# Padding the last 64-token key and query block of each batch to the full 128 x 128 TensorE array

## The chip, the cores and the metric

The kernel runs on one core of one Trainium2 chip. The metric is device time in microseconds (us), lower is better. PE is TensorE, DVE VectorE, ACT ScalarE, POOL GpSimd. PV is the product of the attention weights P with the values v. In the trace a matmul is a weight load (LDWEIGHTS) and a MATMUL. "128*64" is the part of the array it uses: 128 rows (contraction) by 64 columns (output partitions, the width of the loaded weights). The shape behind it, such as 128x65, is the streamed operand: 65 columns.

Single runs of one kernel agree to within about 1%.

## The reference, cut to what matters

Sliding-window attention with an ALiBi bias (8 batches, 8 heads, 576 tokens, head size 64, window 128), then a two-layer feed-forward with squared relu (4608 tokens, 512 to 2048 to 512):

```python
scores = scale * np.matmul(q, k.transpose(0, 1, 3, 2))        # 8 x 8 x 576 x 576
mask = (rel >= 0) & (rel < 128)                               # rel = query pos - key pos
attn = softmax(np.where(mask, scores + bias, -1e9))
x = np.matmul(attn, v) -> reshape to (4608, 512)
out = (np.maximum(x @ w_in, 0) ** 2) @ w_out
```

576 is 4.5 times 128: every batch ends in a block of 64 keys and 64 queries. That half block is the subject.

## The kernel before

A small list scheduler fixes the order of all instructions ahead of time. It interleaves the attention of the coming batches with the feed-forward of tokens already finished. Per batch there are 5 key blocks, the last with n = 64. Cuts are marked with `...`.

```python
blk = [min(128, S - kb * 128) for kb in range(NKB)]          # 128,128,128,128,64
...
for kb in range(NKB):
    n, nq = blk[kb], qcols[kb]
    for c in range(C):                                       # 4 pairs of heads
        nc.tensor.matmul(                                    # scores: n weight columns
            slot.tile[0:n, 0:2 * nq]...,
            kT[p2][c][:, kb * 128:kb * 128 + n],
            qp[p2][c][:, :, kb * 128:kb * 128 + nq], start=True, stop=True)
        # ACT: P = exp(scale * scores) on n partitions; DVE: P = P * masks
    for hf in range(2):
        for hi in range(4):                                  # PV: 8 heads, up to two key blocks each
            for (sp, kk, off) in parts:                      # previous block, this block
                nk = blk[kk]
                nc.tensor.matmul(
                    slot.tile[0:n, hi * (D + 1):(hi + 1) * (D + 1)],
                    sp.tile[0:nk, h, off:off + n],           # weights: nk rows, n columns
                    vt[i][0:nk, kk, h, :], start=st, stop=en)
        # DVE: reciprocal of the row sum, x = pv * reciprocal
    for c in range(C):                                       # transposes of x: n rows
        nc.tensor.transpose(slot.tile[:, c * 128:c * 128 + n],
                            sx.tile[0:n, c * 128:(c + 1) * 128], ident[0:n, 0:n])
```

In the last block of a batch, n = 64 gives 4 score matmuls of form 128*64, 8 PV matmuls of 128*64 (previous key block), 8 PV matmuls of 64*64 (last key block) and 4 transposes of 64*128. That is 24 per batch and 192 in the kernel. P and x come from rotating pools (`work.tile`).

The softmax here doesn't subtract the row's maximum and nothing guards it: scores larger than these inputs give would overflow.

Of the kernel before, what the change touches and what calls it, by code (L numbers as in the profile page):

```python
# [30 lines left out]
class Slot:  # L31


    def __init__(self, tag):
        self.tag, self.tile, self.left, self.freed = tag, None, 0, 0.0


class Plan:
# [17 lines left out]
    def order(self):  # L56
        used = {tag: [] for tag in self.bufs}
        free = {}
        cand = {}
        left = {}  # L60
        for t in self.tasks:
            left[t] = len(t.deps)
            for d in t.deps:
                d.users.append(t)
            for e in t.engs:
                free.setdefault(e, 0.0)
                cand.setdefault(e, [])
        for t in self.tasks:
            if not left[t]:
                for e in t.engs:  # L70
                    cand[e].append(t)

        def avail(t):
            at = t.ready
            for s in t.acq:
                u = used[s.tag]
                n = self.bufs[s.tag]
                if len(u) >= n:
                    old = u[len(u) - n]
                    if old.left:  # L80
                        return None
                    at = max(at, old.freed)
            return at

        done = []
        n_all = len(self.tasks)
        while len(done) < n_all:
            best = None
            for e, c in cand.items():
                lo = None  # L90
                for t in c:
                    a = avail(t)
                    if a is None:
                        continue
                    st = max(a, free[e])
                    k = (st, t.key, t.seq)
                    if lo is None or k < lo[0]:
                        lo = (k, t)
                if lo is not None and (best is None or lo[0][0] < best[0]):
                    best = (lo[0][0], e, lo[1])  # L100
            if best is None:
                raise RuntimeError("plan is stuck: " + repr([
                    (e, t.key, [s.tag for s in t.acq if avail(t) is None]) for e, c in cand.items() for t in c
                    if e != "POOL"][:40]))
            st, e, t = best
            t.eng, t.start = e, st
            dur = t.engs[e]
            if t.dma is not None:
                at = max(st + dur + 900.0, self.dma_free)
                self.dma_free = at + t.dma  # L110
                t.end = self.dma_free + 900.0
            else:
                t.end = st + dur + (self.LAT[e] if t.lat is None else t.lat)
            free[e] = st + dur
            for x in t.engs:
                cand[x].remove(t)
            for s in t.acq:
                used[s.tag].append(s)
            for s in t.rel:
                s.left -= 1  # L120
                s.freed = max(s.freed, t.end)
            for u in t.users:
                left[u] -= 1
                u.ready = max(u.ready, t.end)
                if not left[u]:
                    for x in u.engs:
                        cand[x].append(u)
            done.append(t)
        done.sort(key=lambda t: (t.start, t.seq))
        return done  # L130
# [3 lines left out]
def kernel(  # L134
    ctx: ExitStack, tc: tile.TileContext, q, k, v, moe_w_in, moe_w_out, out
):
    nc = tc.nc
# [8 lines left out]
    NKB = (S + 127) // 128  # L146
    blk = [min(128, S - kb * 128) for kb in range(NKB)]
    qcols = [min(256, S - kb * 128) for kb in range(NKB)]
    C = d_model // 128
    FCB = d_ff // 128  # L150
    NG = NT // 512
# [15 lines left out]
    k8 = const.tile([RP, H, R * D], BF16)  # L167
    vt = [const.tile([128, NKB, H, D + 1], BF16, name=f"vt_{i}") for i in range(NSET)]
    qp = [[const.tile([128, 2, S], BF16, name=f"qp_{i}_{c}") for c in range(C)] for i in range(2)]
    kT = [[const.tile([128, S], BF16, name=f"kT_{i}_{c}") for c in range(C)] for i in range(2)]  # L170

    plan = Plan({"h": 2, "o": 2, "s": 2, "att": 2, "P": 4, "x": 2, "rec": 4, "rt": 3,
                 "g": 2, "osb": 3, "qk": 2, "r8": 3,
                 **{f"{t}{j}": 1 for t in "qk" for j in range(2)},
                 **{f"v{kb}": NSET for kb in range(NKB)}})
# [4 lines left out]
    def dve(n, rate=1):  # L180
        return n / rate / 0.96 + 150.0
# [37 lines left out]
    for i in range(NSET):  # L219
        def ones(i=i):  # L220
            nc.vector.memset(vt[i][:, :, :, D:D + 1], 1.0)
        t_ones.append(plan.add({"DVE": 150.0}, -9e5 + 5, ones))


    def load(key, ns, emit, deps=(), acq=()):
# [59 lines left out]
    def attention(b):  # L285
# [9 lines left out]
        for j in range(2):  # L295
# [13 lines left out]
            for cj in range(2):  # L309
                c = 2 * j + cj  # L310
                t_q[c], t_k[c] = [], []
                for which in ("k", "q"):
# [29 lines left out]
                        lst.append(te)  # L342

                    if which == "k":
                        add_evac(kT[p2][c], [last], 0, 128, t_k[c], {"DVE": dve(576)})
                    else:
                        for c2 in range(2):
                            add_evac(qp[p2][c][c2 * 64:c2 * 64 + 64, c2, :], [last, t_zero[p2][c]], c2 * 64, 64,
                                     t_q[c], {"ACT": act(576)} if c2 else {"DVE": dve(576)})
        P_prev = None  # L350
        for kb in range(NKB):
# [3 lines left out]
            for c in range(C):  # L355
# [3 lines left out]
                def emit(slot=slot, c=c, kb=kb, n=n, nq=nq):  # L359
                    slot.tile = psum.tile([128, 512], FP32, tag="s", name="ps_s")  # L360
                    nc.tensor.matmul(  # L361
                        slot.tile[0:n, 0:2 * nq].rearrange("p (c q) -> p c q", c=2),
                        kT[p2][c][:, kb * 128:kb * 128 + n],
                        qp[p2][c][:, :, kb * 128:kb * 128 + nq],
                        start=True, stop=True)
                final = kb == NKB - 1 and c == C - 1
# [2 lines left out]
                prev_score[:] = [tm]  # L369

                def expo(slot=slot, sP=sP, c=c, n=n, nq=nq):
                    if sP.tile is None:
                        sP.tile = work.tile([128, H, 256], BF16, tag="P", bufs=4, name="P")
                    nc.scalar.activation(  # L374
                        sP.tile[0:n, 2 * c:2 * c + 2, 0:nq],
                        slot.tile[0:n, 0:2 * nq].rearrange("p (c q) -> p c q", c=2),
                        AF.Exp, bias=0.0, scale=scale)
                te = plan.add({"ACT": act(2 * nq)}, ks, expo, [tm], [], [slot])
                if c > 0:
                    te.deps.append(t_P["first"])  # L380
                else:
                    t_P["first"] = te

                def mask(sP=sP, c=c, n=n, nq=nq):
                    pt = sP.tile[0:n, 2 * c:2 * c + 2, 0:nq]
                    nc.vector.tensor_tensor(pt, pt, masks[0:n, 2 * c:2 * c + 2, 0:nq], op=ALU.mult)  # L386
                t_P[c] = plan.add({"DVE": dve(2 * nq, 2)}, ks, mask, [te] + t_mask)

            sx = Slot("x")
# [1 line left out]
            for hf in range(2):  # L391
# [3 lines left out]
                for hi in range(4):  # L395
                    h = 4 * hf + hi
                    parts = ([(P_prev, kb - 1, 128)] if kb else []) + [((sP, t_P), kb, 0)]
                    for pi, ((sp, tp_), kk, off) in enumerate(parts):
                        def emit(slot=slot, sp=sp, kk=kk, off=off, h=h, hi=hi, n=n,
                                 new=hi == 0 and pi == 0, st=pi == 0, en=pi == len(parts) - 1):  # L400
                            if new:
                                slot.tile = psum.tile([128, 512], FP32, tag="att", name="pv")
                            nk = blk[kk]
                            nc.tensor.matmul(  # L404
                                slot.tile[0:n, hi * (D + 1):(hi + 1) * (D + 1)],
                                sp.tile[0:nk, h, off:off + n],
                                vt[i][0:nk, kk, h, :], start=st, stop=en)
                        rel = []
                        if hf == 1 and hi == 3:
                            if off or kb == NKB - 1:  # L410
                                rel += [sp, s_in[b, "v", kk]]
                        last = plan.add({"PE": mm(D + 1)}, kv, emit,
                                        [last, tp_[h // 2], t_vt[b, kk]] + ([t_P[c] for c in range(C)] if hi == 0 and pi == 0 else []),
                                        ([slot] + ([sx] if hf == 0 else [])) if hi == 0 and pi == 0 else [], rel)
                srec = Slot("rec")

# [4 lines left out]
                t1 = plan.add({"DVE": 180.0}, kv, rec, [last], [srec])  # L421

                def norm(slot=slot, srec=srec, sx=sx, hf=hf, n=n):
                    if sx.tile is None:
                        sx.tile = work.tile([128, d_model], BF16, tag="x", bufs=2, name="x")
                    pv = slot.tile[:, 0:4 * (D + 1)].rearrange("p (h e) -> p h e", h=4)
                    nc.vector.tensor_tensor(  # L427
                        sx.tile[0:n, hf * 256:(hf + 1) * 256].rearrange("p (h e) -> p h e", h=4),
                        pv[0:n, :, 0:D],
                        srec.tile[0:n, :].unsqueeze(2).to_broadcast([n, 4, D]),  # L430
                        op=ALU.mult)
# [5 lines left out]
            for c in range(C):  # L437
                def emit(slot=slot, sx=sx, c=c, n=n):
                    if c == 0:
                        slot.tile = psum.tile([128, 1024], BF16, tag="att", name="xp")  # L440
                    nc.tensor.transpose(slot.tile[:, c * 128:c * 128 + n],  # L441
                                        sx.tile[0:n, c * 128:(c + 1) * 128], ident[0:n, 0:n])
                last = plan.add({"PE": mm(n)}, kx, emit, [last, t_norm[1]],
                                [slot] if c == 0 else [], [sx] if c == C - 1 else [])

            def evac(slot=slot, kb=kb, n=n):
# [126 lines left out]
```

## Time and profile before

| | before |
|---|---|
| time, median of 4 runs | 413.48 us (412.85 to 413.69) |
| PE busy | 92% |
| DVE, ACT, POOL busy | 56%, 49%, 17% |
| matmuls of 64 rows or columns | 192 of 2560 |

The page of before, first the busy time of PE, then the 40 slices (tenths of busy time, and of the TensorE clock granted), then the chain of waits that ended last:

```profile
PE 377.1 (92%) x2514; PEld 183.5 (45%) x2560; DVE 230.9 (56%) x610; ACT 200.6 (49%) x381; POOL 71.5 (17%) x97
...
PE   1575799989999999999999999999999999999996
...
PEclk9995569999999999999999999999999999999999
...
PE 83%; DMA 5%; DVE 4%; ACT 3%; POOL 2%; issue 2%; POOLq 0%; ACTq 0%
```

PE is busy from about 60 us to the end, at full clock, and it is most of the chain. (From 30.9 to 58.2 us the granted clock is 0.50; I call this the cold stretch.) So a change helps there only if it shortens PE's own work. (2514 of 2560 matmul records are in this trace; 46 are missing.)

"Busy" does not say that PE streams at full rate. For that, read the starts. This is the PE timeline of before around the last key block of one batch (start us, duration us, engine, line, operation, operands, form, count):

```profile
213.72 0.38 PE L504 MATMUL o<-w_out_sb,g 128*128 128x512 bf16 x1
213.94 0.22 PE L404 MATMUL pv<-vt_72,P 128*128 128x65 bf16 x2
214.09 0.24 PE L361 MATMUL ps_s<-qp_0_74,kT_0_82 128*64 128x128 bf16 x1
214.27 0.60 PE L504 MATMUL o<-w_out_sb,g 128*128 128x512 bf16 x2
214.80 0.24 PE L361 MATMUL ps_s<-qp_1_75,kT_1_83 128*64 128x128 bf16 x1
214.98 0.61 PE L504 MATMUL o<-w_out_sb,g 128*128 128x512 bf16 x2
```

A 128x512 matmul is followed by the next after about 0.217 us, a 65-column PV after about 0.03 us, a full-array matmul of 128 streamed columns after about 0.056 us. Two PV from 213.94 should let the score matmul start at 214.00; it starts at 214.09. The next full matmul should follow at 214.15 and follows at 214.27. The durations of 0.24 us overlap with what comes next and show nothing of this.

The second reading is the weight loads of the short forms, from the groups of instructions by form (busy us, mean ns, then idle time of the weight-load path before them and its cause; "issue" means waiting for nothing that the profile shows):

```profile
L404 PEld LDWEIGHTS <-P 128*128 128x128 bf16 x448 | 38.5, 99 | 35.5 <-issue 6.3 <-DVE x L427 1.5 <-DVE P L386 0.9
...
L404 PEld LDWEIGHTS <-P 128*64 128x64 bf16 x64 | 7.0, 109 | 18.8 <-issue 18.0 <-DVE P L386 0.5
...
L404 PEld LDWEIGHTS <-P 64*64 64x64 bf16 x64 | 6.8, 106 | 18.5 <-issue 18.2
...
L441 PEld LDWEIGHTS <-x 64*128 64x128 bf16 x32 | 3.0, 93 | 9.4 <-issue 7.8 <-DVE P L386 0.8 <-DVE x L427 0.4
```

64 loads of the 128*64 form have 18.0 us of idle "issue" before them, 0.28 us each. 448 full loads have 6.3 us, 0.014 us each.

### The profile page before, as it was taken

The page shows a single profiled execution, that of the slowest core. Times are in us where ns is not written, and L with a number is a line of the kernel's source. Part 1 is how long each engine was busy: PE and PEld are TensorE (multiplying, and loading weights), DVE is VectorE, ACT ScalarE, POOL GpSimd, SP SyncE. Part 2 cuts the span into 40 slices and gives each one's busy share as a digit, 9 for nine tenths or more (in the row PEclk, how much of TensorE's full clock was granted, in tenths as well). Part 3 has the DMA queues.
Part 4 walks back from the last instruction along what each step waited for, and adds up shares of the span by engine and source line. Part 5 has one row for each costly group of instructions (what it writes and reads, how often), then busy time and mean ns, then how long its engine had stood idle before and what let it go on. Part 6 is the DMA issues. An engine that isn't in the chain of part 4 may idle for free.

```text
span 411.5 us, 6496 instructions
## 1 busy us (share of the span) xinstructions
PE 377.1 (92%) x2514; PEld 183.5 (45%) x2560; DVE 230.9 (56%) x610; ACT 200.6 (49%) x381; POOL 71.5 (17%) x97
## 2 busy tenths in 40 slices
PE   1575799989999999999999999999999999999996
PEld 1233434444455444554445445544554443444442
DVE  4786557674686567466666666565755653212200
ACT  1672444545465547265645555555564642344421
POOL 8864313030202020211121020101000000000000
PEclk9995569999999999999999999999999999999999
DMA  7999995566708243742545260423000000010112
GB/s 106 160 204 151 204 104 54 76 100 90 100 5 99 50 81 23 121 53 58 71 78 60 37 74 27 53 38 46 26 27 1 27 26 27 25 53 25 51 53 76
DMA packets 59742, 28.22 MB, mean 69 GB/s; under 512 B 41792, under 2 KB 55104, under 8 KB 59712
## 3 DMA queue, kind: packets, MB, share of 16 engines
q0 software_dynamic: 54528, 18.37, 47.9%
q1 hardware_dynamic: 5184, 9.44, 6.2%
q8 instruction: 20, 0.33, 0.3%
q14 instruction: 10, 0.08, 0.1%
HBM read 36.70 MB, written 9.44 MB: 112 GB/s over the span
## 4 chain that ended last, share of the span: by engine, by line
PE 83%; DMA 5%; DVE 4%; ACT 3%; POOL 2%; issue 2%; POOLq 0%; ACTq 0%
PE h L475 29%; PE o L504 29%; PE pv L404 9%; PE ps_s L361 7%; PE tp L320 5%; DMA k_71<-in_k_dram 3%; PE xp L441 3%; DMA q_70<-in_q_dram 2%; ACT P L374 1%; ACT osb L515 1%; DVE qp_1_79 L334 1%; POOL k_71 L256 1%; ACT qp_1_79 L336 0%; ACT rt L483 0%; DVE qp_2_76 L334 0%
## 5 line engine op out<-in xcount | busy, mean ns | idle before, releaser
L475 PE MATMUL h<-xT,w_in_sb 128*128 128x512 bf16 x549 | 186.3, 383 | 0.8 <-issue 0.2
L504 PE MATMUL o<-w_out_sb,g 128*128 128x512 bf16 x557 | 180.2, 380 | 1.1 <-ACT osb L515 0.3
L483 ACT ACTIVATE rt<-h 128x512 bf16<-128x512 f32 x144 | 85.7, 598 | 84.0 <-PE h L475 68.6
L374 ACT ACTIVATE P<-ps_s 128x512 bf16<-128x512 f32 (+2 forms) x160 | 78.6, 513 | 53.1 <-PE ps_s L361 50.5
L489 DVE TENSOR_TENSOR g<-rt 128x512 bf16<-128x512 bf16 x144 | 59.8, 418 | 59.0 <-ACT rt L483 57.7
L404 PEld LDWEIGHTS <-P 128*128 128x128 bf16 (+1 forms) x576 | 52.2, 100 | 72.8 <-issue 42.6
L504 PEld LDWEIGHTS <-g 128*128 128x128 bf16 x576 | 54.2, 98 | 37.9 <-issue 1.6
L475 PEld LDWEIGHTS <-w_in_sb 128*128 128x128 bf16 x576 | 52.9, 98 | 31.3 <-issue 1.2
L386 DVE TENSOR_TENSOR P<-P,masks 128x512 bf16<-128x512 bf16 (+2 forms) x160 | 55.9, 363 | 18.8 <-ACT P L374 17.0
L404 PE MATMUL pv<-vt_73,P 128*128 128x65 bf16 (+2 forms) x288 | 47.4, 199 | 2.1 <-DVE qp_3_77 L334 0.9
L404 PE MATMUL pv<-vt_72,P 128*128 128x65 bf16 (+2 forms) x288 | 43.9, 203 | 3.6 <-DVE kT_3_89 L334 1.2
L515 ACT ACTIVATE osb<-o 128x512 f32<-128x512 f32 x36 | 21.4, 598 | 37.7 <-PE o L504 37.6
L420 DVE RECIPROCAL rec<-pv 128x4 f32<-128x4 f32 (+1 forms) x80 | 13.4, 176 | 41.9 <-PE pv L404 39.9
L441 PE MATMUL xp<-ident,x 128*128 128x128 bf16 (+1 forms) x160 | 33.5, 220 | 1.2 <-DVE x L427 0.6
L427 DVE TENSOR_TENSOR x<-pv,rec 128x256 bf16<-128x256 f32 (+1 forms) x80 | 32.4, 416 | 0.9
L267 POOL DMA_DIRECT2D vt_73<-in_v_dram x20 | 17.5, 874 | 62.7 <-PE pv L404 37.9
L256 POOL DMA_DIRECT2D q_70<-in_q_dram x16 | 12.3, 768 | 81.9 <-DVE r_2880 L304 11.3
L267 POOL DMA_DIRECT2D vt_72<-in_v_dram x20 | 17.4, 872 | 36.8 <-PE pv L404 28.7
L448 DVE COPY xT<-xp 128x512 bf16<-128x512 bf16 (+1 forms) x40 | 15.8, 396 | 13.3 <-PE xp L441 12.3
L441 PEld LDWEIGHTS <-x 128*128 128x128 bf16 (+1 forms) x160 | 15.5, 99 | 16.0 <-issue 8.7
L256 POOL DMA_DIRECT2D k_71<-in_k_dram x16 | 11.6, 726 | 27.4 <-DVE r_741 L304 10.1
L361 PE MATMUL ps_s<-qp_2_76,kT_2_84 128*128 128x512 bf16 (+2 forms) x20 | 7.2, 360 | 2.5 <-DVE P L386 2.2
(166 smaller groups left out, 317.0 us busy)
## 6 DMA issues: line engine op xcount, KB each, us to landing
out_dram<-osb SPq DMA_DIRECT2D x36, 256.0 KB, 2.0
k_71<-in_k_dram POOLq DMA_DIRECT2D x16, 288.0 KB, 7.1
q_70<-in_q_dram POOLq DMA_DIRECT2D x16, 288.0 KB, 5.7
vt_72<-in_v_dram POOLq DMA_DIRECT2D x16, 128.0 KB, 6.6
w_in_sb<-in_moe_w_in_dram POOLq DMA_DIRECT2D x4, 512.0 KB, 11.4
vt_73<-in_v_dram POOLq DMA_DIRECT2D x16, 128.0 KB, 4.6
w_out_sb<-in_moe_w_out_dram POOLq DMA_DIRECT2D x4, 512.0 KB, 11.4
vt_72<-in_v_dram POOLq DMA_DIRECT2D x4, 64.0 KB, 5.2
```

The lines of the kernel that those rows point to most:

```text
L256: nc.gpsimd.dma_start(dst[:, 4 * j:4 * j + 4, :], src[b, 4 * j:4 * j + 4].rearrange("h (p r) d -> p h (r d)", r=R))
L267: nc.gpsimd.dma_start(vt[i][0:n, kb, :, 0:D], v[b, :, kb * 128:kb * 128 + n, :].rearrange("h s d -> s h d"))
L361: nc.tensor.matmul(slot.tile[0:n, 0:2 * nq].rearrange("p (c q) -> p c q", c=2), kT[p2][c][:, kb * 128:kb * 128 + n], qp[p2][c][:, :, kb * ...
L374: nc.scalar.activation(sP.tile[0:n, 2 * c:2 * c + 2, 0:nq], slot.tile[0:n, 0:2 * nq].rearrange("p (c q) -> p c q", c=2), AF.Exp, bias=0.0, ...
L386: nc.vector.tensor_tensor(pt, pt, masks[0:n, 2 * c:2 * c + 2, 0:nq], op=ALU.mult)
L404: nc.tensor.matmul(slot.tile[0:n, hi * (D + 1):(hi + 1) * (D + 1)], sp.tile[0:nk, h, off:off + n], vt[i][0:nk, kk, h, :], start=st, stop=en)
L427: nc.vector.tensor_tensor(sx.tile[0:n, hf * 256:(hf + 1) * 256].rearrange("p (h e) -> p h e", h=4), pv[0:n, :, 0:D], srec.tile[0:n, :].uns ...
L441: nc.tensor.transpose(slot.tile[:, c * 128:c * 128 + n], sx.tile[0:n, c * 128:(c + 1) * 128], ident[0:n, 0:n])
L475: nc.tensor.matmul(slot.tile, w_in_sb[:, cc, fc * 128:(fc + 1) * 128], xT[:, cc, g * 512:(g + 1) * 512], start=cc == 0, stop=cc == C - 1)
L483: nc.scalar.activation(srt.tile, slot.tile, AF.Relu, bias=0.0, scale=1.0)
L489: nc.vector.tensor_tensor(sg.tile[:, fc, :], srt.tile, srt.tile, op=ALU.mult)
L504: nc.tensor.matmul(slot.tile, sg.tile[:, fc, t * 128:(t + 1) * 128], w_out_sb[:, fc, :], start=fc == 0, stop=fc == FCB - 1)
```

## The change

Intent: with zero keys and zero values behind the last 64 tokens, the last block runs with the same 128-row, 128-column matmuls as all others, and the padded output rows are never read. The tiles that are read beyond what a short block writes (P, x) become persistent, so that they can be cleared once. The core of the diff, cuts marked:

```diff
-    kT = [[const.tile([128, S], BF16, ...
+    kT = [[const.tile([128, SP], BF16, ...                     # SP = 640
+    Pt = [const.tile([128, H, 256], BF16, name=f"P_{i}") for i in range(NP)]     # NP = 4
+    xt = [const.tile([128, d_model], BF16, name=f"x_{i}") for i in range(NX)]    # NX = 2
+        def pad(i=i):                                           # DVE, at the start
+            nc.vector.memset(vt[i][blk[-1]:128, NKB - 1, :, 0:D], 0.0)
+            for c in range(C):
+                nc.vector.memset(kT[i][c][:, S:SP], 0.0)
+    def clear():                                                # POOL, at the start
+        for p in Pt:
+            nc.gpsimd.memset(p[:, :, 192:256], 0.0)
+        for p in xt:
+            nc.gpsimd.memset(p, 0.0)
...
-                        kT[p2][c][:, kb * 128:kb * 128 + n],
+                        kT[p2][c][:, kb * 128:(kb + 1) * 128],
...   exp and mask on 128 partitions instead of n; exp waits for the clear
-                                sp.tile[0:nk, h, off:off + n],
-                                vt[i][0:nk, kk, h, :], start=st, stop=en)
+                                Pt[sp.idx][:, h, off:off + 128],
+                                vt[i][:, kk, h, :], start=st, stop=en)
...
-                    nc.tensor.transpose(slot.tile[:, c * 128:c * 128 + n],
-                                        sx.tile[0:n, c * 128:(c + 1) * 128], ident[0:n, 0:n])
+                    nc.tensor.transpose(slot.tile[:, c * 128:(c + 1) * 128],
+                                        xt[sx.idx][:, c * 128:(c + 1) * 128], ident)
```

More of the change, by code (lines that the diff above doesn't have):

```diff
@@ L34, in __init__ @@
     def __init__(self, tag):
-        self.tag, self.tile, self.left, self.freed = tag, None, 0, 0.0
+        self.tag, self.tile, self.left, self.freed, self.idx = tag, None, 0, 0.0, 0
 class Plan:
@@ L117, in order @@
             for s in t.acq:
+                s.idx = len(used[s.tag]) % self.bufs[s.tag]
                 used[s.tag].append(s)
@@ L148 @@
     qcols = [min(256, S - kb * 128) for kb in range(NKB)]
+    SP = NKB * 128
     C = d_model // 128
@@ L169 @@
     qp = [[const.tile([128, 2, S], BF16, name=f"qp_{i}_{c}") for c in range(C)] for i in range(2)]
-    kT = [[const.tile([128, S], BF16, name=f"kT_{i}_{c}") for c in range(C)] for i in range(2)]
-    plan = Plan({"h": 2, "o": 2, "s": 2, "att": 2, "P": 4, "x": 2, "rec": 4, "rt": 3,
+    kT = [[const.tile([128, SP], BF16, name=f"kT_{i}_{c}") for c in range(C)] for i in range(2)]
+    NP = 4
+    NX = 2
+    Pt = [const.tile([128, H, 256], BF16, name=f"P_{i}") for i in range(NP)]
+    xt = [const.tile([128, d_model], BF16, name=f"x_{i}") for i in range(NX)]
+    plan = Plan({"h": 2, "o": 2, "s": 2, "att": 2, "P": NP, "x": NX, "rec": 4, "rt": 3,
                  "g": 2, "osb": 3, "qk": 2, "r8": 3,
@@ L222 @@
         t_ones.append(plan.add({"DVE": 150.0}, -9e5 + 5, ones))
+    t_pad = []
+    for i in range(2):
+        def pad(i=i):
+            nc.vector.memset(vt[i][blk[-1]:128, NKB - 1, :, 0:D], 0.0)
+            for c in range(C):
+                nc.vector.memset(kT[i][c][:, S:SP], 0.0)
+        t_pad.append(plan.add({"DVE": 400.0}, -9e5 + 6, pad))
+    def clear():
[3 more added lines that the diff above has]
+            nc.gpsimd.memset(p, 0.0)
+    t_clear = plan.add({"POOL": 3000.0}, -9e5 + 1, clear)
     def load(key, ns, emit, deps=(), acq=()):
@@ L344, in attention @@
                     if which == "k":
-                        add_evac(kT[p2][c], [last], 0, 128, t_k[c], {"DVE": dve(576)})
+                        add_evac(kT[p2][c][:, 0:S], [last, t_pad[p2]], 0, 128, t_k[c], {"DVE": dve(576)})
                     else:
@@ L361, in emit @@
                     nc.tensor.matmul(
-                        slot.tile[0:n, 0:2 * nq].rearrange("p (c q) -> p c q", c=2),
-                        kT[p2][c][:, kb * 128:kb * 128 + n],
+                        slot.tile[:, 0:2 * nq].rearrange("p (c q) -> p c q", c=2),
+                        kT[p2][c][:, kb * 128:(kb + 1) * 128],
                         qp[p2][c][:, :, kb * 128:kb * 128 + nq],
@@ L371, in expo @@
                 def expo(slot=slot, sP=sP, c=c, n=n, nq=nq):
-                    if sP.tile is None:
-                        sP.tile = work.tile([128, H, 256], BF16, tag="P", bufs=4, name="P")
                     nc.scalar.activation(
-                        sP.tile[0:n, 2 * c:2 * c + 2, 0:nq],
-                        slot.tile[0:n, 0:2 * nq].rearrange("p (c q) -> p c q", c=2),
+                        Pt[sP.idx][:, 2 * c:2 * c + 2, 0:nq],
+                        slot.tile[:, 0:2 * nq].rearrange("p (c q) -> p c q", c=2),
                         AF.Exp, bias=0.0, scale=scale)
-                te = plan.add({"ACT": act(2 * nq)}, ks, expo, [tm], [], [slot])
+                te = plan.add({"ACT": act(2 * nq)}, ks, expo, [tm, t_clear], [], [slot])
                 if c > 0:
@@ L384, in mask @@
                 def mask(sP=sP, c=c, n=n, nq=nq):
-                    pt = sP.tile[0:n, 2 * c:2 * c + 2, 0:nq]
-                    nc.vector.tensor_tensor(pt, pt, masks[0:n, 2 * c:2 * c + 2, 0:nq], op=ALU.mult)
+                    pt = Pt[sP.idx][:, 2 * c:2 * c + 2, 0:nq]
+                    nc.vector.tensor_tensor(pt, pt, masks[:, 2 * c:2 * c + 2, 0:nq], op=ALU.mult)
                 t_P[c] = plan.add({"DVE": dve(2 * nq, 2)}, ks, mask, [te] + t_mask)
@@ L402, in emit @@
                                 slot.tile = psum.tile([128, 512], FP32, tag="att", name="pv")
-                            nk = blk[kk]
                             nc.tensor.matmul(
-                                slot.tile[0:n, hi * (D + 1):(hi + 1) * (D + 1)],
-                                sp.tile[0:nk, h, off:off + n],
-                                vt[i][0:nk, kk, h, :], start=st, stop=en)
+                                slot.tile[:, hi * (D + 1):(hi + 1) * (D + 1)],
+                                Pt[sp.idx][:, h, off:off + 128],
+                                vt[i][:, kk, h, :], start=st, stop=en)
                         rel = []
@@ L412, in attention @@
                         last = plan.add({"PE": mm(D + 1)}, kv, emit,
-                                        [last, tp_[h // 2], t_vt[b, kk]] + ([t_P[c] for c in range(C)] if hi == 0 and pi == 0 else []),
+                                        [last, tp_[h // 2], t_vt[b, kk], t_pad[i]] + ([t_P[c] for c in range(C)] if hi == 0 and pi == 0 else []),
                                         ([slot] + ([sx] if hf == 0 else [])) if hi == 0 and pi == 0 else [], rel)
@@ L423, in norm @@
                 def norm(slot=slot, srec=srec, sx=sx, hf=hf, n=n):
-                    if sx.tile is None:
-                        sx.tile = work.tile([128, d_model], BF16, tag="x", bufs=2, name="x")
                     pv = slot.tile[:, 0:4 * (D + 1)].rearrange("p (h e) -> p h e", h=4)
                     nc.vector.tensor_tensor(
-                        sx.tile[0:n, hf * 256:(hf + 1) * 256].rearrange("p (h e) -> p h e", h=4),
+                        xt[sx.idx][0:n, hf * 256:(hf + 1) * 256].rearrange("p (h e) -> p h e", h=4),
                         pv[0:n, :, 0:D],
@@ L440, in emit @@
                         slot.tile = psum.tile([128, 1024], BF16, tag="att", name="xp")
-                    nc.tensor.transpose(slot.tile[:, c * 128:c * 128 + n],
-                                        sx.tile[0:n, c * 128:(c + 1) * 128], ident[0:n, 0:n])
-                last = plan.add({"PE": mm(n)}, kx, emit, [last, t_norm[1]],
+                    nc.tensor.transpose(slot.tile[:, c * 128:(c + 1) * 128],
+                                        xt[sx.idx][:, c * 128:(c + 1) * 128], ident)
+                last = plan.add({"PE": mm(128)}, kx, emit, [last, t_norm[1], t_clear],
                                 [slot] if c == 0 else [], [sx] if c == C - 1 else [])
```

## The prediction

> **What bounds the kernel now.** TensorE: page part 1 shows PE busy 92% (DVE 56%, ACT 49%), the chain of waits PE 83%, and the slices PE at 9 tenths from 60 us to the end at full clock. The list of waits shows the others waiting for PE (relu<-h matmuls 68.6 us, square<-relu 57.7 us).
>
> **What the padding removes.** PE busy hides it, but start-to-start times in the PE timeline show it. Full-array neighbours follow at streaming rate: a 128x512 matmul every 0.217 us, a 65-column PV every 0.03 us, a 72-row transpose 0.035 us. Around a matmul with 64 array rows or columns this breaks. Before the 128*64 score matmul at 214.09 about 0.09 us is lost, and the next starts 0.18 us after it instead of 0.06; the same at 214.80, 215.51, 216.07. Over all pairs after 55 us I read a median loss of 94-98 ns going in and 102-120 ns coming out, about 0.21 us per matmul, for 128*64, 64*64 and 64*128 alike; 72*128 loses nothing. Weight loads agree: PV loads of 64 columns show 18 us of idle "issue" per form. The Trainium skill, "TensorEngine Tiling (Array Packing)", section Tiling Modes/Key Properties, says that changing tiling mode drains the TensorE; this trace agrees, at about 0.21 us per round trip.
> Per batch there are 4 score, 16 PV and 4 transpose matmuls of this kind: 24 x 8 = 192, nearly all alone between full ones. About 180 run after 53 us, where PE is the limit: 180 x 0.21 = 38 us. The changed kernel has none left.
>
> **What it adds.** Transposes stream 128 instead of 64 columns: 32 x 26 ns = 0.8 us. Scores and PV stream the same. Exp and mask on 128 partitions keep their free size, so 269 and 213 ns should stay. At the start POOL gets six memsets, some 0.6 us each by its present 64x576 memsets, 3.6 us, ahead of the weight loads and batch 1's loads; POOL is on the chain there (to 22 us, then the 12.4 us landing of k). DVE gets ten small memsets, about 2 us, mostly before k arrives at 6.2 us.
>
> **Sum.** Steady part -38 + 0.8 us. In 45-60 us PE runs at clock 0.50 and is the chain; 12 padded matmuls there save about 3 us. The POOL memsets cost 1 to 3.6 us, partly hidden because DMA is backed up (205 GB/s flat in 18-30 us). With PE 12% faster, DVE rises to about 75% in 60-340 us and some 2 us come back as PE waits. Net about -38 us: 375.5 us.
>
> **Chances.** Range 368 to 384 (8 in 10). Faster by over 2%: 0.97; within 2%: 0.02; slower: 0.01.
>
> **What the profile would show.** Right: no 64-row/64-column forms; each drain closes to 0.03-0.06 us spacing; each 40 us stretch of 60-345 us loses about 5 us; means of h and o matmuls (383, 380 ns) unchanged or a little lower; PE idle near zero in the middle; POOL's k load for batch 1 issued 3 us later than 19.8 us.
> Wrong: matmuls after a padded one still start late; or PE gains turn into waits for ACT/DVE evictions or for k, q, v loads.
>
> **What would make it wrong.** The loss is not the shape switch but these matmuls' dependence on late P (then it stays); the start slips by over 4 us because weight loads and batch 1 queue behind the memsets; the cold clock lasts beyond 58 us; another interleaving of the static order, or dependencies of the persistent tiles adding waits between ACT, DVE and PE.

## The result, and the profile after

| | before | after |
|---|---|---|
| time, median | 413.48 us (4 runs) | 377.78 us (4 runs, 377.25 to 379.92) |
| ratio, 95% interval | | 0.9149 (0.9111 to 0.9186) |
| PE, DVE, ACT busy | 92%, 56%, 49% | 91%, 61%, 53% |

A later series of five runs of the changed kernel gave 378.36 us and a ratio of 0.9158 (0.9145 to 0.9170). The profiled run of after is its slowest, 379.92 us; differences of a microsecond or two between profiled spans are not used below. The page of after, the same lines as before:

```profile
PE 343.4 (91%) x2560; PEld 178.6 (47%) x2560; DVE 231.6 (61%) x620; ACT 199.7 (53%) x381; POOL 75.1 (20%) x103
...
PE   0567589989999999999999999999999999999995
...
PEclk9998569999999999999999999999999999999999
...
PE 79%; DVE 10%; ACT 6%; DMA 2%; issue 2%; POOL 0%; ACTq 0%; POOLq 0%
```

PE is about as full as before (91% against 92%): its busy share hardly fell, the span did. The PE timeline of after at the same place in the work, the scores of the last key block of the same batch:

```profile
199.61 0.19 PE L424 MATMUL pv<-vt_72,P_92 128*128 128x65 bf16 x1
199.64 0.22 PE L384 MATMUL ps_s<-qp_0_74,kT_0_82 128*128 128x128 bf16 x1
199.69 0.38 PE L522 MATMUL o<-w_out_sb,g 128*128 128x512 bf16 x1
199.91 0.22 PE L384 MATMUL ps_s<-qp_1_75,kT_1_83 128*128 128x128 bf16 x1
199.97 0.59 PE L522 MATMUL o<-w_out_sb,g 128*128 128x512 bf16 x2
200.40 0.22 PE L384 MATMUL ps_s<-qp_2_76,kT_2_84 128*128 128x128 bf16 x1
```

The score matmul now starts 0.03 us after a PV, and the next one 0.05 to 0.06 us after the score. Both gaps are gone. The PV weight loads by form, now one group per P tile, of which one is shown:

```profile
L424 PEld LDWEIGHTS <-P_90 128*128 128x128 bf16 x144 | 13.9, 102 | 11.4 <-issue 2.9 <-DVE P_90 L407 0.4
```

The four groups of 144 loads hold 9.6 us of "issue" in all (2.9 + 2.2 + 1.0 + 3.5), where before the PV loads held 42.5 us (6.3 + 18.0 + 18.2).

From the starts of all matmuls one can account for the span. For each pair of neighbours I took the start-to-start time and subtracted the usual distance of the first one's form (0.216 us for 512 streamed columns, 0.163 for 384, 0.056 for 128, 0.03 for 65 and 72). The loss is the number of 64-row and 64-column matmuls times the median of what is left before and after one of them; all the rest are waits. From 53 us to the last matmul:

| | before | after |
|---|---|---|
| streaming | 305.5 us | 306.5 us |
| loss at 174 short matmuls (0.211 us each) | 36.7 us | 0 |
| waits | 12.1 us | 14.1 us |
| sum | 354.3 us | 320.6 us |

(In before, the 46 missing records are counted as streaming at 0.216 us, and the waits are the remainder.) The median loss was 94 to 98 ns going into a short form, and coming out 102 ns after 64*128, 117 ns after 64*64 and 120 ns after 128*64, hence 0.211 us.

The waits from 53 us on also hold some of the cold stretch, which ends at 58.2 us in before and at 54.6 us in after. Counted anew from 60 us on, at full clock in both, the waits are about 10 us in before and 13 us in after.

### The profile page after: what moved, and what is told of

Its sections match the earlier page's. It is cut to its first block, busy times and chain, and to the rows that moved or that the text cites. A ratio compares the mean times of both kernels' runs of the same rounds, so it can differ in the third digit from the quotient of the medians.

```text
span 378.2 us, 6568 instructions
## 1 busy us (share of the span) xinstructions
PE 343.4 (91%) x2560; PEld 178.6 (47%) x2560; DVE 231.6 (61%) x620; ACT 199.7 (53%) x381; POOL 75.1 (20%) x103
## 4 chain that ended last, share of the span: by engine, by line
PE 79%; DVE 10%; ACT 6%; DMA 2%; issue 2%; POOL 0%; ACTq 0%; POOLq 0%
PE o L522 31%; PE h L493 29%; PE ps_s L384 7%; PE pv L424 5%; PE tp L343 4%; DMA k_71<-in_k_dram 2%; PE xp L459 2%; ACT P_91 L395 1%; DVE qp_1_75 L357 1%; DVE qp_2_76 L357 1%; DVE qp_0_74 L357 1%; ACT qp_2_76 L359 1%; ACT rt L501 1%; DVE qp_1_79 L357 1%; DVE qp_0_78 L357 1%
## 5 line engine op out<-in xcount | busy, mean ns | idle before, releaser
L493 PE MATMUL h<-xT,w_in_sb 128*128 128x512 bf16 x576 | 188.4, 380 | 0.1
L522 PE MATMUL o<-w_out_sb,g 128*128 128x512 bf16 x576 | 183.6, 379 | 0.5 <-ACT osb L533 0.3
L395 ACT ACTIVATE P_91<-ps_s 128x512 bf16<-128x512 f32 (+2 forms) x40 | 20.0, 515 | 10.5 <-PE ps_s L384 10.2
L395 ACT ACTIVATE P_93<-ps_s 128x512 bf16<-128x512 f32 (+2 forms) x40 | 19.5, 516 | 9.2 <-PE ps_s L384 8.9
L395 ACT ACTIVATE P_92<-ps_s 128x512 bf16<-128x512 f32 (+2 forms) x40 | 19.5, 515 | 7.1 <-PE ps_s L384 6.3
L395 ACT ACTIVATE P_90<-ps_s 128x512 bf16<-128x512 f32 (+2 forms) x40 | 19.4, 516 | 5.5 <-PE ps_s L384 5.0
L424 PEld LDWEIGHTS <-P_93 128*128 128x128 bf16 x144 | 13.7, 101 | 12.7 <-issue 3.5
L424 PEld LDWEIGHTS <-P_90 128*128 128x128 bf16 x144 | 13.9, 102 | 11.4 <-issue 2.9
L424 PEld LDWEIGHTS <-P_91 128*128 128x128 bf16 x144 | 13.6, 100 | 11.4 <-issue 2.2
L424 PEld LDWEIGHTS <-P_92 128*128 128x128 bf16 x144 | 13.4, 99 | 10.2 <-issue 1.0
L459 PE MATMUL xp<-ident,x_94 128*128 128x128 bf16 x80 | 17.2, 227 | 0.7 <-DVE x_94 L445 0.6
L407 DVE TENSOR_TENSOR P_91<-P_91,masks 128x512 bf16<-128x512 bf16 (+2 forms) x40 | 14.0, 363 | 5.7 <-ACT P_91 L395 5.3
```

The costliest lines, as they stand in the source:

```text
L395: nc.scalar.activation(Pt[sP.idx][:, 2 * c:2 * c + 2, 0:nq], slot.tile[:, 0:2 * nq].rearrange("p (c q) -> p c q", c=2), AF.Exp, bias=0.0, ...
L424: nc.tensor.matmul(slot.tile[:, hi * (D + 1):(hi + 1) * (D + 1)], Pt[sp.idx][:, h, off:off + 128], vt[i][:, kk, h, :], start=st, stop=en)
L459: nc.tensor.transpose(slot.tile[:, c * 128:(c + 1) * 128], xt[sx.idx][:, c * 128:(c + 1) * 128], ident)
L493: nc.tensor.matmul(slot.tile, w_in_sb[:, cc, fc * 128:(fc + 1) * 128], xT[:, cc, g * 512:(g + 1) * 512], start=cc == 0, stop=cc == C - 1)
L522: nc.tensor.matmul(slot.tile, sg.tile[:, fc, t * 128:(t + 1) * 128], w_out_sb[:, fc, :], start=fc == 0, stop=fc == FCB - 1)
```

## The experiments

Twelve runs, all correct. Each is after with the edit shown; e10 is after itself, run again.

### Was it the padding, and which part? (e1 to e4)

The theory is that each matmul with 64 rows or 64 columns makes the array drain, that is finish what it holds, on the way in and out. First rival: the persistent tiles did it, by taking away buffer waits or changing the static order. Second rival: these matmuls are slow because their P comes late, whatever their shape. e1 takes all padding of matmuls away and keeps the rest:

```diff
-                        kT[p2][c][:, kb * 128:(kb + 1) * 128],
+                        kT[p2][c][:, kb * 128:kb * 128 + n],
-                                Pt[sp.idx][:, h, off:off + 128],
-                                vt[i][:, kk, h, :], start=st, stop=en)
+                                Pt[sp.idx][0:blk[kk], h, off:off + n],
+                                vt[i][0:blk[kk], kk, h, :], start=st, stop=en)
-                                        xt[sx.idx][:, c * 128:(c + 1) * 128], ident)
+                                        xt[sx.idx][0:n, c * 128:(c + 1) * 128], ident[0:n, 0:n])
```

(and outputs, exp and mask cut to n in the same way). e2, e3 and e4 leave one of the three paddings in.

> After, with every score, PV and transpose matmul of the last block cut back to 64 rows or columns; persistent P and x tiles, pads and clears stay. Shape-switch theory: all 192 short matmuls are back, each with about 0.21 us of loss, and the clears at the start cost about 2 to 3 us, so 413 to 417 us. Rival (the gain came from the persistent tiles, through fewer buffer waits or another static order): stays below 390 us.

> As e1, but the 32 score matmuls of the last blocks padded to 128 keys. Shape-switch theory: 32 x 0.21 = 6.7 us less than e1. Rival (late P, that is the wait of these matmuls for exp and mask): no gain, within 1.5 us of e1.

> As e1, but only the 128 PV matmuls of the last blocks run with 128 rows and 128 columns. Shape-switch theory: 128 x 0.21 = 27 us less than e1, two thirds of the whole gain. Rival (late P): P is produced as late as in e1, so no gain.

> As e1, but only the 32 transposes of x padded to 128 rows. Shape-switch theory: 32 x 0.20 us less the 0.8 us of longer streaming, 5 to 6 us less than e1. With e2 and e3 the three gains should add up to about 39 us if each matmul pays on its own; if a few places of the order are to blame they need not add.

| run | median us | ratio to before, 95% | less than e1 | per matmul |
|---|---|---|---|---|
| e1 tiles, clears and pads only | 415.33 | 1.0059 (1.0037 to 1.0082) | | |
| e2 32 scores padded | 409.64 | 0.9922 (0.9899 to 0.9946) | 5.7 us | 0.18 us |
| e3 128 PV padded | 387.33 | 0.9389 (0.9353 to 0.9426) | 28.0 us | 0.22 us |
| e4 32 transposes padded | 410.62 | 0.9944 (0.9910 to 0.9978) | 4.7 us | 0.15 us |
| after: all 192 | 377.78 | 0.9149 | 37.6 us | 0.20 us |

The first rival falls: the tiles with their clears and pads make the kernel 2.2 us slower (415.33 against 413.12 us in the same rounds). The second falls with e3, in which P is produced by the same steps as in e1 and only the PV form differs, yet 28.0 us go. The three gains add up to 38.4 us against 37.6 us for all together. So each matmul pays for itself, close to the 0.21 us read from the gaps. The transposes give back some of it for streaming 128 columns in place of 64. Scores and transposes gained up to 1 us less than I had expected.

The last column is less exact than it looks, because the cold stretch differs too. It ends at 60.9 us in e1, 57.3 in e2, 50.7 in e3, 59.6 in e4 and 54.6 in after. After the first feed-forward matmul e1 still runs 6.2 us at half clock and e3 none, so an estimated 3 us (half of the 6.2) of e3's 28.0 us is the clock, which leaves about 0.20 us for each PV; of the 37.6 us for all together it is an estimated 2 us. No run separates this clock gain from the padding. The 0.211 us from the starts is free of it: the same medians, within 1 ns, come out of the pairs after 60 us alone.

### What makes a form short: the tiling mode or the weight load? (e5)

Third rival: the loss is in the weight load. The Trainium skill, "TensorE: Matmul & The Clock Gate", section "Weight-path perf modes", says that the fast weight load is on when the number of weights is 128 and the type is not FP32. A padding to only 96 keys, rows and columns is more than half the array but not 128 columns:

```diff
-                                slot.tile[:, hi * (D + 1):(hi + 1) * (D + 1)],
-                                Pt[sp.idx][:, h, off:off + 128],
+                                slot.tile[0:(128 if n == 128 else 96), hi * (D + 1):(hi + 1) * (D + 1)],
+                                Pt[sp.idx][0:(128 if blk[kk] == 128 else 96), h, off:off + (128 if n == 128 else 96)],
```

> After, but scores and PV of the last block padded only to 96 keys, 96 rows and 96 columns; transposes full. Tiling-mode theory (more than 64 rows and columns use the whole array, so no drain): within 3 us of after, 376 to 381 us, no 0.09 us loss ahead of a 96-column matmul. Rival (the fast weight load needs all 128 columns, and its absence is what costs): the 160 matmuls with 96 columns lose as much as with 64, 405 to 412 us.

Measured: 378.85 us, ratio 0.9166 (0.9136 to 0.9195), the same as after. Its weight-load groups by form, then its PE timeline at a 96-column score:

```profile
L424 PEld LDWEIGHTS <-P 96*96 96x96 bf16 x64 | 8.4, 131 | 4.0 <-issue 0.6
...
L424 PEld LDWEIGHTS <-P 128*96 128x96 bf16 x64 | 8.3, 130 | 4.0 <-issue 0.4
```

```profile
197.78 0.22 PE L424 MATMUL pv<-vt,P 128*128 128x65 bf16 x2
197.84 0.23 PE L384 MATMUL ps_s<-qp,kT 128*96 128x128 bf16 x1
197.91 0.38 PE L522 MATMUL o<-w_out_sb,g 128*128 128x512 bf16 x1
```

The 96-column weight load is slower than the full one (130 against about 100 ns), and slower even than the 64-column load of before (106 to 109 ns). Still nothing is lost: the score starts 0.06 us after two PV, and the next matmul 0.07 us later. The slow 96-column load is hidden under the matmul before it. The trace agrees with the skill's page as far as the loads with fewer than 128 columns are the slower ones here (130 and 106 to 109 against about 100 ns), but that is not the cause of the loss.

### Is it paid per matmul or per switch? (e6)

If it is a switch of mode, eight short matmuls in a row pay once. These three runs start from after (scores and transposes full) and change only PV in the last block: 128 rows, 64 columns, either spread as the static order has them or all eight of a half emitted in one piece; and the pieces with 128 columns, as a control.

```diff
 # spread
-                                Pt[sp.idx][:, h, off:off + 128],
+                                Pt[sp.idx][:, h, off:off + n],
 # grouped: one scheduler task for a half of the last block, in place of eight
+                if kb == NKB - 1:
+                    def group(...):
+                        for hi in range(4):
+                            for pi, (sp, kk, off) in enumerate([(sp0, NKB - 2, 128), (sp1, NKB - 1, 0)]):
+                                nc.tensor.matmul(slot.tile[0:n, ...], Pt[sp.idx][:, 4 * hf + hi, off:off + n],
+                                                 vt[i][:, kk, 4 * hf + hi, :], start=pi == 0, stop=pi == 1)
+                    last = plan.add({"PE": 8 * mm(D + 1)}, kv, group, ...)
```

> After, but the 128 PV matmuls of the last blocks write 64 columns again, with all 128 rows, each where the static order puts it, between others. If a short column count alone costs the full 0.21 us: 128 x 0.21 = 27 us more than after, about 405 us. If rows and columns each cost half: about 391 us.

> As e6_cols64_spread, but the eight PV matmuls of a half (4 heads x 2 key blocks, all 128 rows x 64 columns) are emitted in one piece, 16 pieces in all. Switch theory: the loss is paid going into and out of a piece, 16 x 0.21 = 3.4 us, plus some 0.03 to 0.07 us for each weight load not hidden: 381 to 390 us. Rival (each short matmul pays by itself, in its weight load): no gain over spread, about 405 us.

> Control for the grouping: as e6_cols64_grouped with 128 columns. Grouping by itself should change little: 376 to 381 us.

| run | median us | ratio to before, 95% |
|---|---|---|
| 64 columns, spread | 406.14 | 0.9825 (0.9800 to 0.9849) |
| 64 columns, grouped | 378.74 | 0.9158 (0.9131 to 0.9186) |
| 128 columns, grouped | 375.93 | 0.9090 (0.9070 to 0.9109) |

The PV weight loads of the short form, first in the spread run, then in the grouped one, and the PE timeline of one group:

```profile
L424 PEld LDWEIGHTS <-P 128*64 128x64 bf16 x128 | 13.6, 110 | 37.2 <-issue 36.4 <-DVE P L407 0.5
```

```profile
L421 PEld LDWEIGHTS <-P 128*64 128x64 bf16 x128 | 5.8, 116 | 4.2 <-issue 3.5 <-DVE x L458 0.5
```

```profile
211.03 0.38 PE L506 MATMUL h<-xT,w_in_sb 128*128 128x512 bf16 x1
211.34 0.44 PE L421 MATMUL pv<-vt,P 128*64 128x65 bf16 x8
211.71 0.21 PE L343 MATMUL tp<-ident,r 72*128 72x72 bf16 x1
```

This decides it. The same 128 short matmuls cost 28.4 us spread (against after) and 2.8 us grouped (against the grouped control), 0.18 us for each of the 16 groups. (Spread ends its cold stretch at 60.0 us and after at 54.6, so an estimated 2 to 3 us of the 28.4 is the clock; the grouped pair ends it at 52.9 and 53.0 us.) Inside a group one short matmul follows the other after 0.030 us in the median, as full ones of 65 columns do. In the timeline the group starts 0.09 us later than the 0.217 us of the matmul before it, and its eight take 0.37 us to the next start, of which 0.24 us is streaming. So a matmul of 64 columns is not slow; going over to it and back is. The Trainium skill, "TensorEngine Tiling (Array Packing)", section "Tiling Modes", says so without a price: changing the tiling mode drains the TensorE. (That a matmul of 64 rows or columns counts as another mode is inferred; no record names the mode.) And all 128 rows with 64 columns pay in full, so the column count alone is enough; the 64*128 transposes of before show the same for rows alone. The two do not add: 64*64 loses no more than 128*64.

One rival e5 leaves open: that the loss is the 0.1 us of a weight load which is not hidden at a switch. The starts of the weight loads settle it. These are the loads of before at the score matmul of 214.09 and at the one that follows it at 214.27:

```profile
214.09 0.11 PEld L361 LDWEIGHTS <-kT_0_82 128*64 128x64 bf16 x1
214.26 0.11 PEld L504 LDWEIGHTS <-g 128*128 128x128 bf16 x2
```

Between full matmuls a load starts 2 ns after the start of the matmul before it, so it runs ahead of its own matmul. At a switch it does not. In the spread run, in which no record is missing, the load of a short PV begins a median 92 ns after the matmul before it has streamed, and the PV starts 2 ns after its load. So the lost time lies before the load, not in it: first the wait, then load and matmul together.

The grouped run came in below the 381 to 390 us that I expected, since in the group no weight load was left uncovered, and the control just below its 376 to 381. The control is 2 us below after, with only the order of the instructions changed. Its waits from 53 us on, counted as in the table above, are 10.7 us against 14.1. Why this order waits less was not followed up.

### What the start costs (e7 to e10)

The changed kernel begins later. In after the second copy of k on DVE and the clears on POOL ran at the same time. The same copy in the DVE timeline of before, then in that of after, then the clears in the POOL timeline of after:

```profile
11.08 0.79 DVE L304 COPY r_145<-k_71 72x2048 bf16<-72x2048 bf16 x1 [2.02 <-DMA k_71<-in_k_dram]
```

```profile
11.21 3.08 DVE L327 COPY r_161<-k_71 72x2048 bf16<-72x2048 bf16 x1 [1.84 <-DMA k_71<-in_k_dram]
```

```profile
10.90 0.52 POOL L242 MEMSET P_90<- 128x512 bf16 x1
11.36 0.52 POOL L242 MEMSET P_91<- 128x512 bf16 x1
...
13.23 0.52 POOL L244 MEMSET x_95<- 128x512 bf16 x1
```

The copy takes 3.08 us in place of 0.79 and ends at 14.29, about 0.5 us after the last memset. In e2 the order is the other way round: the copy is quick, and the four memsets of P, 0.47 us apart where nothing disturbs them, take 2.46 us in place of 1.92 (DVE timeline, then POOL timeline, of e2):

```profile
11.62 0.98 DVE L327 COPY r<-k 72x2048 bf16<-72x2048 bf16 x1 [2.54 <-DMA k<-in_k_dram]
```

```profile
10.61 2.46 POOL L242 MEMSET P<- 128x512 bf16 x4
```

So in each run with the six clears one of the two bears most of the wait: either the copy takes 2.05 to 3.08 us, or one or two memsets take 1.07 us in place of 0.52 and the copy only 0.89 to 1.19. The Trainium skill, "SBUF — State Buffer", section "SBUF: two separate sides", has this as an exclusive lock of a port pair shared by DVE and GpSimd; these traces agree with it. In the static order of after, the first exp stands behind the clears, the building of the masks and two query copies; it comes at 21.39 us, against 13.87.

e7 keeps the one clear that is needed (P tile 3, the only one read before it was ever written) and moves it behind batch 1's loads. e8 is e7 with the PV groups of 128 columns. e9 also moves eight older POOL memsets, of the second query buffers, behind these loads.

```diff
-        for p in Pt:
-            nc.gpsimd.memset(p[:, :, 192:256], 0.0)
-        for p in xt:
-            nc.gpsimd.memset(p, 0.0)
-    t_clear = plan.add({"POOL": 3000.0}, -9e5 + 1, clear)
+        nc.gpsimd.memset(Pt[3][:, :, 192:256], 0.0)
+    t_clear = plan.add({"POOL": 500.0}, -6.5e5, clear)
-                te = plan.add(..., expo, [tm, t_clear], [], [slot])
+                te = plan.add(..., expo, [tm] + ([t_clear] if kb == 3 and b == 0 else []), [], [slot])
 # e9 only: key of the second buffers' zero memsets
-                                    -9e5 + 4 if i == 0 else -75e4, zero)
+                                    -9e5 + 4 if i == 0 else -65e4, zero)
```

> After, with one POOL memset (the fourth P buffer, the only one read before it was ever written) instead of six, placed after batch 1's loads; exp no longer waits for it, except in the fourth block of batch 0. Theory: the six memsets cost the start 2 to 3 us, in the load issues behind them, in the exp waits, and in the DVE copy of the second k half, which took 3.08 us beside them in after and 0.79 us in before; expected 374.5 to 376.5 us, that copy under 1.3 us, first exp near 14 us instead of 21.4. Rival (the lag at the start is hidden later, since loads and the cold clock set the pace until 55 us): within 1 us of after.

> e7 and the grouping of e6_cols128_grouped together, in search of the fastest version. If the two gains are independent (e6_cols128_grouped stands 2 us below after): 372 to 374.5 us. If both only shorten the same start: no better than the better one of the two, 375 us.

> e8, and the eight POOL memsets of the second query buffers (4.9 us on POOL, on the chain before batch 1's loads) moved behind those loads. If the issue time of batch 1's loads sets the start: 3 to 5 us below e8. If the DMA engines, flat at 205 GB/s in 18 to 30 us, set it: 0 to 1.5 us below e8.

> The changed kernel itself once more, to set e7 against more runs of it: the four runs so far lie between 377.25 and 379.92 us. If e7 (376.65 us) is really faster by the 1 us its medians show, this gives a median of 377.5 to 378.5 us; if the start's cost is hidden, 376 to 377 us. In the profile: the DVE copy of the second k half either waits for the six POOL memsets (over 2 us, ending about 0.5 us after the last of them) or runs in about 1 us and one memset of 0.52 us takes about 1.05 us instead.

| run | median us | ratio to before, 95% | second k copy | first exp at |
|---|---|---|---|---|
| e10, after again (5 runs) | 378.36 | 0.9158 (0.9145 to 0.9170) | 2.57 us | 21.10 us |
| e7 small clear | 376.65 | 0.9116 (0.9094 to 0.9139) | 0.69 us | 14.41 us |
| e8 small clear, grouped | 374.92 | 0.9071 (0.9056 to 0.9086) | 0.79 us | 13.89 us |
| e9 as e8, late zeros | 375.81 | 0.9090 (0.9071 to 0.9110) | 0.69 us | 14.48 us |

Against its first four runs e7 could not be told from after (the intervals overlapped), which is why after was run again: now they do not overlap, and e7 is 1.7 us faster by the medians. It missed the 374.5 to 376.5 us that I expected by a little. Most of the seven microseconds of exp did not reach the end of the kernel. In the profiled runs of e7, e8 and e9 the cold stretch is also shorter, 17.1 us against 20.5 in after, so a part of their gain may be the clock; no run separates it. e9 was a miss that tells something: batch 1's k load is issued at 15.58 us against 19.67 in e8, yet it landed at 30.63 us against 28.97, and the first kT copy from it comes at 33.69 us against 33.12. The DMA engines were flat at about 205 GB/s from 20 to 30 us, so issuing earlier did not land earlier. e8 is the fastest version found, faster than both kernels. Its 374.92 us is nearer to the case in which its two parts only shorten the same start (375) than to that of independent gains (372 to 374.5); of the two parts, it is not separated from the grouped control alone (0.9090, intervals overlap).

## Why the prediction was right

The time (375.5 us predicted, 368 to 384; 377.78 measured): right, and so was the main mechanism. The smaller terms were right in size but in part for other reasons. Point by point:

- **0.21 us of drain per short matmul, 180 of them, 38 us.** Right. The account gives 174 after 53 us and 36.7 us; e1 against after gives 37.6 us for all 192, e3 0.22 us per PV. That it is a switch was taken from the skill; e6 shows it, and e5 with the starts of the loads excludes the weight load.
- **Streaming +0.8 us.** The account has +1.0 us.
- **Some 2 us come back as PE waits.** Right in size: 12.1 to 14.1 us. That DVE's higher share did it is not shown: counted from 60 us on, the waits are about 10 us in before and 13 in after, but also 13 in the spread run, in which PE is nearly as slow as in before, and 11 in the grouped control. They follow the static order at least as much. The DVE share in 60 to 300 us came to 70% (168.5 us busy of 240), and to 65% in the 60 to 340 us that I had named, not 75%. The page's chain moved from PE 83% to 79%, with DVE 10% where it had 4%.
- **Exp and mask on 128 partitions cost the same.** Right: groups of 275 to 280 ns and 216 to 220 ns, against 269 and 213 before.
- **The clears cost 1 to 3.6 us.** Right as a size (e1: 2.2 us over before), wrong as a path. I counted POOL time ahead of the loads, and the k load of batch 1 was indeed issued 2.4 us later, at 22.21 us in place of 19.77. But it landed no later, at 29.11 us against 29.62, so the loads did not carry the cost. The DVE copy that waits out the memsets, and the exp that slips by 7.5 us, were not foreseen.
- **The cold stretch saves about 3 us.** In size about right: batch 1's first kT copy is 3.1 us late (37.35 against 34.28), and the first feed-forward matmul only 0.6 us (52.98 against 52.41). e1, with the clears and without the padding, separates the two. From the one to the other it takes 18.1 us, as before does, and after takes 15.6, all at clock 0.50: the padding saved 2.5 us there. By that matmul the clears had cost 2.3 us (54.72 in e1). Not foreseen: full clock comes back at 54.6 us in place of 58.2, an estimated 2 us more (5.8 us at half clock after the first feed-forward matmul in before, 1.7 in after, half of the difference).
- **The sum.** A slip in arithmetic: my own terms, -38 + 0.8 - 3 + (1 to 3.6) + 2, add up to -34.6 to -37.2 us, not to the -38 that I wrote. The measured -35.7 us lies inside. That it lies so close is partly luck, since the earlier clock was not in the sum and the waits and the clears came about in other ways than I wrote.

## What to carry to other kernels

A lone matmul that uses 64 of the array's rows or columns, standing between full ones, cost about 0.21 us here, whether 64, 65 or 128 columns streamed through it; fewer than 64 were not tested. Padding it to more than half (96 was enough) removes the cost, and putting such matmuls of one form next to each other leaves one cost for the group. Look for it in start-to-start times and in "issue" idle time before weight loads of the short form, since PE busy hides it. Initial clears are not free either: check which are really read before they are written, and keep POOL memsets away from DVE copies on the critical path.

## What the Trainium skill lacked or had wrong

- "TensorEngine Tiling (Array Packing)": it says that changing the tiling mode drains the TensorE, with no price. Here 94 to 98 ns going in and 102 to 120 ns coming out, at full clock, and nothing between equal forms (0.030 us from start to start); spread, 128 such matmuls cost 28 us of 406, of which an estimated 2 to 3 us is the clock. Its advice to tile for contraction or column counts of 64 or less lacks the warning that a single short matmul among full ones loses.
- The same page calls 64 or less small and lists tile sizes of 32, 64 and 128, but does not say how sizes between 64 and 128 run. Here 72 rows (transposes) and 96 rows or columns lose nothing beside full ones (0 to 5 ns in the median).
- "TensorE: Matmul & The Clock Gate": its section "LDWEIGHTS (loading the stationary operand)" puts a load at the number of columns / 1.2 in ns, an estimate of 107 ns for 128 columns, 80 for 96 and 53 for 64. Here a 96-column load took 123 to 131 ns and a 64-column one 106 to 110 ns, against 97 to 102 ns for 128, so the narrower loads took longer; the slower load was hidden (e5: 378.85 us).
- "SBUF — State Buffer": the lock is described per instruction, going to whichever starts first. With a queue of POOL memsets the DVE copy was kept out over several of them (2.05 to 3.08 us in six runs with the six clears: after, e1, e10 and the three of e6), and in others (e2, e3, e4, e5) it got in between and one or two memsets took 0.5 us longer. The page doesn't say which engine gets the lock when both stand in line.
